# Grouped-query attention: one more chunk of scores exponentiated bank by bank, and VectorE's share of the exponentials begun three chunks earlier and ended three chunks later

## The chip, the cores and the metric

The kernel runs on one core of a Trainium2 chip. The metric is the device time of one execution in microseconds (us), the median of several executions.

## The reference

```
B, Hq, Hkv, Sq, Sk, D = 16, 32, 8, 288, 512, 128      # bf16
k, v = repeat(k, 4, axis=1), repeat(v, 4, axis=1)
p = softmax(einsum("bhqd,bhkd->bhqk", q, k) * D ** -0.5)
out = einsum("bhqk,bhkd->bhqd", p, v)
```

## The kernel before

There are 128 groups (batch x key head), each with 1152 queries against 512 keys. A group is cut into three chunks of 128 x 1536 scores, 384 chunks in all, numbered from 0. A chunk fills three banks of the matmul accumulator (PSUM). For chunk n, TensorE makes the scores; ScalarE exponentiates them into on-chip memory (SBUF); two chunks later TensorE multiplies with V, twelve matmuls that I call PV(n), with a column of ones in V for the denominators; VectorE divides and evicts. GpSimd copies each group's V, as it was transferred, into the layout with the column of ones.

In every sixth chunk VectorE exponentiates the last 120 columns itself, with eight instructions, and ScalarE gets 1416 columns. I call such chunks shared. The first chunks (and the last) go through ScalarE bank by bank, so that TensorE can go on before a whole chunk is done. The parts:

```
FIRST = 2            # chunks exponentiated bank by bank at the start
FIRST_SHARED = 6     # first shared chunk
EVERY = 6
...
def shared(n):
    return FIRST_SHARED <= n < NS - NC and (n - FIRST_SHARED) % EVERY == 0   # NS = 384, NC = 3
...
def op_exp(n):                       # ScalarE
    parts = [(0, CH)]                            # CH = 1536
    if shared(n):
        parts = [(0, CH - W)]                    # W = 120
    if n < FIRST or n == NS - 1:
        parts = [(x, x + BANK) for x in range(0, CH, BANK)]
    ...
def op_vc(g):                        # GpSimd: V of group g
    waits = [have("v", g)]                       # its transfer
    if g >= 2:
        waits.append(("s_pv", NC * (g - 2) + 2)) # PV of the second chunk of group g-2
    emit(eng, waits, lambda: eng.tensor_copy(v_sb[...], vd_sb[...]))
...
for r in range(NS - 1):              # VectorE, n = r + LAG, LAG = 2
    op_rc(r)                                     # reciprocals after PV(r)
    if shared(n):     op_y(n)                    # clamp, from PSUM
    if shared(n - 1): op_yu(n - 1, 1); op_yu(n - 1, 2); op_yp(n - 1)
    op_ev(r)                                     # eviction of r
    if shared(n):     op_yb(n); op_ym(n); op_yu(n, 0)   # from SBUF to SBUF
```

PV(r) waits, among others, for the eviction of r - 2, whose buffer it takes.

## Time and profile before

| | before |
|---|---|
| time, median | 521.98 us (521.74 to 523.07, 3 runs) |
| span of the profiled run | 520.0 us |
| busy: TensorE, ScalarE, VectorE, GpSimd | 98%, 99%, 71%, 15% |
| six chunks in the body | 7.982 us |

A period of six chunks is the repeating unit. I read it from the starts of TensorE's weight loads: the scores of chunk 13 begin at 21.69 us, those of chunk 373 at 500.64, and 478.95/60 = 7.982. The lines of the profile that carry the argument stand in the prediction below.

### The profile page before, as it was taken

The page shows a single profiled execution, that of the slowest core. Times are in us where ns is not written, and L with a number is a line of the kernel's source. Part 1 is how long each engine was busy: PE and PEld are TensorE (multiplying, and loading weights), DVE is VectorE, ACT ScalarE, POOL GpSimd, SP SyncE. Part 2 cuts the span into 40 slices and gives each one's busy share as a digit, 9 for nine tenths or more (in the row PEclk, how much of TensorE's full clock was granted, in tenths as well). Part 3 has the DMA queues.
Part 4 walks back from the last instruction along what each step waited for, and adds up shares of the span by engine and source line. Part 5 has one row for each costly group of instructions (what it writes and reads, how often), then busy time and mean ns, then how long its engine had stood idle before and what let it go on. Part 6 is the DMA issues. An engine that isn't in the chain of part 4 may idle for free.

```text
span 520.0 us, 15243 instructions
## 1 busy us (share of the span) xinstructions
PE 510.3 (98%) x6118; PEld 394.6 (76%) x6224; DVE 369.6 (71%) x1315; ACT 513.3 (99%) x393; POOL 79.8 (15%) x135
## 2 busy tenths in 40 slices
PE   8999999999999999999999999999999999999997
PEld 5777777777777777777777777777777777777776
DVE  2767767777777677676776776767767767677776
ACT  7999999999999999999999999999999999999997
POOL 2111111111111111111111111111111111111110
PEclk9999999999999999999999999999999999999999
DMA  9999999999999998999999989999998989998212
GB/s 186 237 218 230 267 194 248 225 213 210 219 233 256 208 245 201 235 248 240 215 241 209 209 225 220 241 185 209 229 240 232 227 194 201 192 234 198 86 69 93
DMA packets 253078, 110.06 MB, mean 212 GB/s; under 512 B 219728, under 2 KB 236752, under 8 KB 253008
## 3 DMA queue, kind: packets, MB, share of 16 engines
q1 hardware_dynamic: 252720, 108.82, 97.7%
q8 instruction: 49, 0.80, 0.7%
q10 hardware_dynamic: 288, 0.26, 0.2%
q14 instruction: 21, 0.17, 0.2%
HBM read 17.04 MB, written 37.75 MB: 105 GB/s over the span
## 4 chain that ended last, share of the span: by engine, by line
ACT 98%; DMA 1%; issue 1%; DVE 0%; PE 0%
ACT pt_sb L516 97%; DMA qt_sb<-in_q_dram 1%; ACT pt_sb L511 1%; PE ps_s L439 0%; DVE o_sb L585 0%; DVE o_sb L595 0%; PE ps_s L479 0%; DVE rl_sb L575 0%; PE ps_o L669 0%; DVE bad_sb L621 0%; DVE flag_i L734 0%; DVE bad_sb L618 0%
## 5 line engine op out<-in xcount | busy, mean ns | idle before, releaser
L516 ACT ACTIVATE pt_sb<-ps_s 128x1536 bf16<-128x1536 f32 (+2 forms) x384 | 508.8, 1441 | 0.0
L479 PE MATMUL ps_o<-v_sb,pt_sb 128*128 128x129 bf16 x4584 | 322.3, 220 | 1.1
L479 PEld LDWEIGHTS ps_o<-v_sb,pt_sb 128*128 128x128 bf16 x4584 | 282.8, 98 | 49.7 <-DVE o_sb L585 14.1
L439 PE MATMUL ps_s<-qt_sb,kt_sb 128*128 128x512 bf16 (+2 forms) x1430 | 290.4, 320 | 5.0 <-DMA qt_sb<-in_q_dram 0.5
L585 DVE TENSOR_TENSOR o_sb<-ps_o,rl_sb 128x384 bf16<-128x384 f32 x382 | 211.9, 555 | 9.3 <-DVE rl_sb L575 0.5
L439 PEld LDWEIGHTS ps_s<-qt_sb,kt_sb 128*128 128x128 bf16 x1536 | 123.9, 98 | 62.3 <-issue 1.1
L575 DVE RECIPROCAL rl_sb<-ps_o 128x3 f32<-128x3 f32 x382 | 68.1, 178 | 125.5 <-PE ps_o L479 124.0
L568 POOL COPY v_sb<-vd_sb 128x512 bf16<-128x512 bf16 x128 | 78.8, 616 | 429.1 <-PE ps_o L479 408.9
L549 DVE SCALAR_TENSOR_TENSOR u_sb<-u_sb,m_sb 128x120 f32<-128x120 f32 x126 | 35.6, 283 | 2.2
L556 DVE SCALAR_TENSOR_TENSOR pt_sb<-u_sb,e_sb 128x120 bf16<-128x120 f32 x63 | 17.8, 283 | 2.2
L549 DVE SCALAR_TENSOR_TENSOR u_sb<-m_sb 128x120 f32<-128x120 f32 x63 | 17.4, 277 | 0.0
L527 DVE TENSOR_SCALAR y_sb<-ps_o 128x120 f32<-128x120 f32 x63 | 15.9, 253 | 0.0
L540 DVE TENSOR_SCALAR m_sb<-t_sb 128x120 int32<-128x120 int32 x63 | 14.1, 223 | 2.2
L540 DVE TENSOR_SCALAR e_sb<-t_sb 128x120 int32<-128x120 int32 x63 | 13.6, 216 | 0.0
L450 PE MATMUL ps_o<-qt_sb,kt_sb 128*128 128x120 bf16 x63 | 13.6, 216 | 0.0
L533 DVE TENSOR_SCALAR t_sb<-y_sb 128x120 int32<-128x120 f32 x63 | 13.4, 213 | 0.0
L450 PEld LDWEIGHTS ps_o<-qt_sb,kt_sb 128*128 128x128 bf16 x63 | 6.2, 98 | 7.4
L511 ACT ACTIVATE pt_sb<-ps_s 128x512 bf16<-128x512 f32 x6 | 3.3, 616 | 2.3 <-PE ps_s L439 2.3
L411 DVE COPY kt_sb<-ps_o 128x128 bf16<-128x128 bf16 (+2 forms) x3 | 1.0, 336 | 6.2 <-PE ps_o L404 6.1
L613 DVE TENSOR_REDUCE st_sb<-rl_sb 128x1 f32<-128x72 f32 (+1 forms) x16 | 3.5, 216 | 0.0
L611 DVE TENSOR_REDUCE st_sb<-rl_sb 128x1 f32<-128x72 f32 (+1 forms) x16 | 3.5, 216 | 0.0
L417 PE MATMUL ps_o<-const-bfloat16-1.0 128*128 128x512 bf16 (+1 forms) x6 | 2.4, 570 | 0.9 <-PEq L752 0.9
(32 smaller groups left out, 12.0 us busy)
## 6 DMA issues: line engine op xcount, KB each, us to landing
out_dram<-o_sb SPq DMA_DIRECT2D x127, 288.0 KB, 3.7
vd_sb<-in_v_dram SPq DMA_DIRECT2D x31, 512.0 KB, 5.5
qt_sb<-in_q_dram SPq DMA_TRANSPOSE x128, 4.9
kt_sb<-in_k_dram SPq DMA_TRANSPOSE x32, 5.1
vd_sb<-in_v_dram SPq DMA_DIRECT2D x1, 384.0 KB, 4.6
out_dram<-o_sb SPq DMA_DIRECT2D x3, 96.0 KB, 1.6
kd_sb<-in_k_dram ACTq DMA_DIRECT2D x2, 128.0 KB, 2.7
vd_sb<-in_v_dram SPq DMA_DIRECT2D x1, 128.0 KB, 3.3
```

The lines of the kernel that those rows point to most:

```text
L439: ins = emit(eng, w_x, lambda: eng.matmul(ps_s[:, n % 2, c:c + w], kt_sb[:, sl, j, gi, :], qg[:, t * P:t * P + w], start=True, stop=True))
L450: emit(eng, [("s_ev", n - LAG - 1)], lambda: eng.matmul(ps_o[:, (n - LAG) % 2, BANK - W:BANK], kt_sb[:, (g // UG) % NSLOT, j, g % UG, :], ...
L479: ins = emit(eng, w_x, lambda: eng.matmul(outs(r)[:, t - r % NC * TPC, :], pt(g, t, j), v_sb[:, sl, gi * NJ + j, 0:DV], start=(x == 0), st ...
L516: emit(eng, waits, lambda: eng.activation(d, s, ACTF.Exp, scale=scale)).then_inc(sem["s_e"], 1)
L527: emit(eng, [("s_yb", nth(n) - NB), ("s_pv", n - LAG + 1)], lambda: eng.tensor_scalar(out=y_sb[:, b], in0=ps_o[:, (n - LAG) % 2, BANK - W: ...
L533: emit(eng, [("s_ym", 2 * (nth(n) - NB)), ("s_y", nth(n))], lambda: eng.tensor_scalar(out=t_sb[:, b], in0=y_sb[:, b], scalar1=Y_MUL, scala ...
L540: emit(eng, [("s_yp", nth(n) - NB), ("s_yb", nth(n))], lambda: eng.tensor_scalar(out=dst[:, b], in0=t_sb[:, b], scalar1=mask, scalar2=bits ...
L549: lambda: eng.scalar_tensor_tensor(out=u_sb[:, b, x], in0=src, scalar=QUARTIC[x], in1=m, op0=ALU.add, op1=ALU.mult)
L556: lambda: eng.scalar_tensor_tensor(out=pt_sb[:, n % NPT, CH - W:CH], in0=u_sb[:, b, 2], scalar=QUARTIC[3], in1=e_sb[:, b].bitcast(FP32), o ...
L568: emit(eng, waits, lambda: eng.tensor_copy(v_sb[:, sl, gi * NJ:(gi + 1) * NJ, 0:D], vd_sb[:, sl, gi].rearrange("p (j d) -> p j d", d=D))). ...
L575: emit(eng, [("s_pv", r + 1)], lambda: eng.reciprocal(rl_sb[:, TPC * r:TPC * (r + 1)].unsqueeze(2), outs(r)[:, :, D:DV])).then_inc(sem["s_ ...
L585: emit(eng, waits, lambda: eng.tensor_tensor(out=o_sb[:, g % NO, t0:t0 + TPC, :], in0=outs(r)[:, :, 0:D], in1=rl_sb[:, TPC * r:TPC * (r + ...
```

## The change

Two constants and one bound. The intent: chunk 2 lets TensorE go on sooner, and sharing begins at chunk 3 and ends at chunk 381, so ScalarE is relieved once more and earlier.

```diff
-    FIRST = 2
-    FIRST_SHARED = 6
+    FIRST = 3
+    FIRST_SHARED = 3
...
-            return FIRST_SHARED <= n < NS - NC and (n - FIRST_SHARED) % EVERY == 0
+            return FIRST_SHARED <= n < NS - 2 and (n - FIRST_SHARED) % EVERY == 0
```

## The prediction

> **What bounds the kernel now.** The work goes in 384 chunks of 128x1536 scores. For chunk n TensorE makes the scores (L439), ScalarE exponentiates them (L516), and two chunks later TensorE multiplies with V (L479). In every sixth chunk VectorE exponentiates the last 120 columns, so ScalarE gets 1416. I call chunks by number from 0; "PV(n)" is the product with V of chunk n.
>
> I read the page first. Its busy shares do not decide, and its chain names ScalarE:
>
> ```profile
> PE 510.3 (98%) x6118; PEld 394.6 (76%) x6224; DVE 369.6 (71%) x1315; ACT 513.3 (99%) x393; POOL 79.8 (15%) x135
> ...
> ACT 98%; DMA 1%; issue 1%; DVE 0%; PE 0%
> ```
>
> Two engines at 98 and 99% with nothing idle cannot both be the limit, so I looked at when instructions start, which the timeline of each engine gives. First ScalarE, from three windows of its timeline (start, length of the merged piece, how many instructions):
>
> ```profile
> 5.05 1.09 ACT L511 ACTIVATE pt_sb<-ps_s 128x512 bf16<-128x512 f32 x2 [2.33 <-PE ps_s L439]
> 6.02 0.60 ACT L516 ACTIVATE pt_sb<-ps_s 128x512 bf16<-128x512 f32 x1
> 6.50 1.10 ACT L511 ACTIVATE pt_sb<-ps_s 128x512 bf16<-128x512 f32 x2
> ...
> 7.93 2.85 ACT L516 ACTIVATE pt_sb<-ps_s 128x1536 bf16<-128x1536 f32 x2
> 10.59 2.88 ACT L516 ACTIVATE pt_sb<-ps_s 128x1536 bf16<-128x1536 f32 x2
> 13.26 2.80 ACT L516 ACTIVATE pt_sb<-ps_s 128x1416 bf16<-128x1416 f32 x2
> 15.95 2.79 ACT L516 ACTIVATE pt_sb<-ps_s 128x1536 bf16<-128x1536 f32 x2
> ```
>
> Chunks 0 and 1 go bank by bank: six pieces between 5.05 and 7.93 are 0.48 us from start to start. Chunks 2 to 5 start at 7.93, 9.26, 10.59, 11.93: 1.333 us each. So a piece of c columns costs ScalarE a fixed 0.053 us plus c x 0.833 ns when nothing holds it up (from (1.333 - 0.48)/1024 and the rest). By that, a chunk of 1416 takes 1.233 us (estimate). But chunks 6 and 7, the first of them short, take 15.95 - 13.26 = 2.69 us, where 1.233 + 1.333 = 2.57 would do: **ScalarE waits about 0.12 us after the short chunk.** A period of six chunks needs 5 x 1.333 + 1.233 = 7.90 us of ScalarE and takes
>
> ```profile
> 13.26 7.97 ACT pt_sb L516 x6
> 21.28 7.93 ACT pt_sb L516 x6
> ...
> 476.28 7.93 ACT pt_sb L516 x6
> ```
>
> (the chain of waits in order of time) (476.28 - 21.28)/57 = 7.982 us. So ScalarE has 0.08 us to spare in each period. What sets 7.982 is TensorE. Its timeline:
>
> ```profile
> 8.31 0.81 PE L439 MATMUL ps_s<-qt_sb,kt_sb 128*128 128x512 bf16 x3
> 8.96 0.94 PE L479 MATMUL ps_o<-v_sb,pt_sb 128*128 128x129 bf16 x12
> ...
> 13.04 0.88 PE L479 MATMUL ps_o<-v_sb,pt_sb 128*128 128x129 bf16 x12
> 13.76 0.81 PE L439 MATMUL ps_s<-qt_sb,kt_sb 128*128 128x512 bf16 x2
> 14.41 0.84 PE L479 MATMUL ps_o<-v_sb,pt_sb 128*128 128x129 bf16 x12
> 15.09 0.82 PE L439 MATMUL ps_s<-qt_sb,kt_sb 128*128 128x512 bf16 x6
> 15.74 0.84 PE L479 MATMUL ps_o<-v_sb,pt_sb 128*128 128x129 bf16 x12
> ```
>
> From 13.76 on it alternates 0.65 and 0.68 us without a gap: 1.33 us per chunk, six of them 7.98. An unhindered PV shows a length of 0.84. In the body all do; the two longer ones near the start, 0.94 and 0.88, are stalls of 0.10 and 0.04 us. The first is PV(1), whose last four matmuls need chunk 2 (they use its first two banks) and which waits for the whole exponential of chunk 2, ending 7.93 + 1.51 = 9.44; the second is PV(4), which waits in the same way for chunk 5 (11.93 + 1.54 = 13.47). **So: ScalarE bounds chunks 0 to 5, TensorE everything from about 13.7 us to the end.** At the very end PV(382) shows 1.11 instead of 0.84, a stall of 0.27 us on the second bank of chunk 383.
>
> **What the Trainium skill says.** "TensorE: Matmul & The Clock Gate", section "Back-to-back issue gap", gives N/2.4 + 2.5 ns for a warm matmul alone: 56.3 ns at 129 columns, 215.8 at 512. Then a chunk is 12 x 56.3 + 3 x 215.8 = 1323 ns; the trace has 1330. The trace agrees within 1%, and not with the shorter gap for long streams that the section also gives (131 ns at 512). "ScalarE: Activation LUTs", "What ACT_TABLE_LOAD costs", gives 186 ns + 0.833 ns per column for an ACTIVATE and an overlap of about 93 ns with its neighbour; slope and the length of a single bank agree (613 ns; the trace has 616), but the overlap here is 616 - 480 = 136 ns, and I use that. "Perfetto Trace Analysis", "Identifying the Most-Contended Engine", says that matmul occupancy does not tell how near TensorE is to its limit; that is why I read starts and not the 98%.
>
> **The change part by part.**
> 1. *Chunk 2 in three pieces.* ScalarE: 3 x 0.48 = 1.44 instead of 1.333, so +0.107 us, in the stretch that ScalarE bounds. TensorE: PV(1) may use the first two banks when they are done, at about 7.93 + 2 x 0.48 + 0.14 = 9.03 instead of 9.44, and needs them at 8.96 + 8 x 0.056 = 9.41: its stall of 0.10 goes. Scores of chunk 4 may overwrite bank by bank, too.
> 2. *The first shared chunk is 3, not 6.* ScalarE: -0.10 us at chunk 3, +0.10 at chunk 6. Sum for chunk 5: it starts at 7.93 + 1.44 + 1.233 + 1.333 = 11.94, before 11.93. So PV(4) waits for chunk 5 until the same moment as before. What PV(1) no longer waits is waited at PV(4): its stall grows from 0.04 to about 0.12-0.14. The scores of chunk 7 start at 13.76 before and at 13.76-13.77 after. **Gain at the start: 0.00 +- 0.03 us.** From there ScalarE starts chunk 7 at 14.60 at the earliest (13.27 + 1.333), where the scores let it start at 14.61; chunk 9 then gives it its slack.
> 3. *VectorE's work.* Shared chunks were 6 to 378 (63), now 3 to 381 (64): one more extra matmul (the same 120 columns, split off; +2.5 ns by the formula) and one more set of eight VectorE instructions: 0.25 + 0.21 + 0.22 + 0.22 + 0.28 + 2 x 0.28 + 0.28, about 2.0 us, on an engine with 29% to spare. In chunk 6, from VectorE's reading at 14.06 to its last result takes 2.4 us and the two delayed evictions end by 16.91 and 17.59, the next reciprocal coming at 17.95 on time; PV(7), which waits for the first of them, starts at 17.07 with 0.16 in hand. The same distances hold for chunk 3. There the reciprocal follows PV(1), ending near 9.80, and the eviction that PV(4) needs ends near 12.79, before 12.95.
> 4. *The end.* Chunk 381 being short gives ScalarE 0.10 us, but chunk 383 starts at 514.87, while its scores (issued 513.99, some 0.86 to ScalarE's start) allow 514.86: gain 0.01. The two evictions delayed by chunk 381's work would end at 515.8 and 516.5 instead of 515.0 and 516.3, and the reciprocal after PV(382) comes at about 516.47 either way, so the last stores hardly move: 0 to +0.05.
>
> One more short chunk is worth 0.10 us of ScalarE that TensorE does not let through. Sum: 0.00 (start) + 0.00 (body, TensorE's 1.33 per chunk is untouched) - 0.01 to +0.05 (end): about 0.0 us, 0.01% at most. I say 521.9 us, the median of before within its scatter.
>
> **The rivals.** (a) *ScalarE is the bound*, as the chain's 98% says: then 64 short chunks instead of 63 give -0.10, two more fixed costs +0.107, again zero, so the time does not tell the two apart; the chain does not either, since it follows ScalarE whenever that shows no idle time. (b) *TensorE keeps what PV(1) wins:* 0.10 to 0.13 us less, 521.85, if chunk 5 came earlier than I add up; the starts at 1.333 speak against. (c) *VectorE late:* if chunk 3's work held up PV(4) or chunk 381's the last evictions, 0.1 to 0.6 us more; for it speaks only the margin of 0.16. (d) *Phase:* shared chunks now fall on the other buffer of scores and apart from VectorE's reductions of every 24 chunks, whose period before (37.21 to 45.19) is as long as its neighbours, 7.98. So that gains nothing. Only a repeating effect could matter: 0.02 us in each of 64 periods would be 1.3 us, and even that is 0.25%.
>
> **Range and chances.** Three runs of before spread from 521.74 to 523.07, more than all terms above together. The range is 521.3 to 522.8: scatter on both sides and a tenth or two for (b) or (c). 2% is 10.4 us, a hundred times the largest term: within 2% 0.985, faster 0.01, slower 0.005.
>
> **What would show it.** PV(1) at 0.84 instead of 0.94; PV(4) at 0.95-0.98 instead of 0.88; scores of chunk 7 at 13.76 +- 0.03; chunk 3 starting near 9.37, chunk 5 near 11.94; periods of 7.98 in the body; PV(382) still near 1.1. Periods of 7.95 or 8.02 would prove the argument on the body wrong, PV(4) at 0.84 that on the start.

## The result, and the profile after

The changed kernel took 522.25 us (521.9 to 522.8, 4 runs), the kernel before 521.86 (521.69 to 523.07, 4 runs). The ratio of the fast runs is 1.0003, 95% interval 0.9986 to 1.0021: no difference by timing. The span of the profiled run went from 520.0 to 520.6 us.

The page of the changed kernel, engines' busy time and the chain that ended last:

```profile
PE 510.1 (98%) x6119; PEld 394.4 (76%) x6225; DVE 371.4 (71%) x1323; ACT 513.7 (99%) x395; POOL 79.8 (15%) x135
...
PE 96%; DVE 2%; issue 1%; DMA 1%
```

The busy shares are as before. The chain now runs through TensorE (96%), where before it ran through ScalarE (98%), though the time is the same. That is the sign of two engines near one limit: the chain takes whichever shows no gap, and tells little about which one binds.

TensorE's timeline in the changed kernel (start, length of the merged piece, how many):

```profile
7.72 0.40 PE L404 MATMUL ps_o<-ident,kd_sb 128*128 128x128 bf16 x4 [0.65 <-DMA kd_sb<-in_k_dram]
...
8.73 0.76 PE L439 MATMUL ps_s<-qt_sb,kt_sb 128*128 128x512 bf16 x3
9.32 0.21 PE L450 MATMUL ps_o<-qt_sb,kt_sb 128*128 128x120 bf16 x1
9.38 0.84 PE L479 MATMUL ps_o<-v_sb,pt_sb 128*128 128x129 bf16 x12
...
13.37 0.84 PE L479 MATMUL ps_o<-v_sb,pt_sb 128*128 128x129 bf16 x12
...
20.70 0.81 PE L439 MATMUL ps_s<-qt_sb,kt_sb 128*128 128x512 bf16 x3
21.66 0.85 PE L479 MATMUL ps_o<-v_sb,pt_sb 128*128 128x129 bf16 x12
```

Three things are to be seen. PV(1), at 9.38, is back at 0.84 us, as predicted (e2 will show that this need not be the pieces' doing). PV(4), at 13.37, is at 0.84 as well, where I had predicted a stall: TensorE had to wait for the second block of keys until 7.72 us (7.30 in the trace before), so it came too late to wait for ScalarE. And there is a gap that I had not predicted: the scores of chunk 12 start at 20.70 and need 0.65, so PV(10) could start at 21.35, but starts at 21.66. What held it, from the timeline of all engines:

```profile
19.39 0.66 POOL L568 COPY v_sb<-vd_sb 128x512 bf16<-128x512 bf16 x1 [4.50 <-DMA vd_sb<-in_v_dram]
19.49 0.69 DVE L549 SCALAR_TENSOR_TENSOR u_sb<-m_sb 128x120 f32<-128x120 f32 x1
...
21.05 0.55 DVE L585 TENSOR_TENSOR o_sb<-ps_o,rl_sb 128x384 bf16<-128x384 f32 x1
...
21.65 0.68 PEld L479 LDWEIGHTS ps_o<-v_sb,pt_sb 128*128 128x128 bf16 x12 [0.64 <-DVE o_sb L585]
```

PV(10) waits for the eviction that ends at 21.60. That eviction stands in VectorE's order behind the work for shared chunk 9, in which one instruction took 0.69 us that takes 0.28 elsewhere. It began while GpSimd copied V. In the kernel before no chunk is in work on VectorE at that moment; its copy at 19.54 harmed nothing.

So the theory to test was this. **Theory C:** starting the sharing earlier puts VectorE's work of chunks 3 and 9 where GpSimd's first copies of V fall, which follow the arrival of transfers and not the rhythm of the loop, and the two engines hold each other up. **Rival N:** that was chance. **Rival V:** VectorE's extra work alone is too long at the start. And for the body: **theory T**, TensorE bounds it, against **R**, ScalarE does.

### The profile page after: what moved, and what is told of

Its sections match the earlier page's. It is cut to its first block, busy times and chain, and to the rows that moved or that the text cites. A ratio compares the mean times of both kernels' runs of the same rounds, so it can differ in the third digit from the quotient of the medians.

```text
span 520.6 us, 15257 instructions
## 1 busy us (share of the span) xinstructions
PE 510.1 (98%) x6119; PEld 394.4 (76%) x6225; DVE 371.4 (71%) x1323; ACT 513.7 (99%) x395; POOL 79.8 (15%) x135
## 4 chain that ended last, share of the span: by engine, by line
PE 96%; DVE 2%; issue 1%; DMA 1%
PE ps_o L479 50%; PE ps_s L439 45%; DMA kd_sb<-in_k_dram 1%; PE ps_o L450 1%; PE ps_o L417 0%; DVE o_sb L585 0%; DVE u_sb L549 0%; PE ps_o L404 0%; DVE rl_sb L575 0%; DVE pt_sb L556 0%; DVE m_sb L540 0%; DVE o_sb L595 0%; DVE kt_sb L411 0%; DVE t_sb L533 0%; DVE y_sb L527 0%
## 5 line engine op out<-in xcount | busy, mean ns | idle before, releaser
L511 ACT ACTIVATE pt_sb<-ps_s 128x512 bf16<-128x512 f32 x8 | 4.4, 618 | 2.3 <-PE ps_s L439 2.3
```

## The experiments

Twelve runs were made. Two of them repeat a kernel (e1 and e12), and all but e6 gave right results. "Before" is the kernel before on the same chip. "Keys" is when TensorE began with the second block of keys; "3 to 13" the time from the scores of chunk 3 to those of chunk 13, which is 13.31 when nothing stalls; the last column one period of six chunks, from chunk 13 to 373. These three come from the starts of TensorE's weight loads in the one trace of each run. "Keys" follows the arrival of these keys, except in e7 and e11, where they landed at 7.76 and 5.93 us and TensorE came to them later.

| run | time | before | ratio (95%) | keys | 3 to 13 | six chunks |
|---|---|---|---|---|---|---|
| kernel before | | | | 7.30 | 13.41 | 7.982 |
| changed kernel | 522.25 | 521.86 | 1.0003 (0.9986, 1.0021) | 7.72 | 13.59 | 7.983 |
| e1 changed, again | 522.25 | 521.66 | 1.0011 (0.9997, 1.0025) | 7.38 | 13.99 | 7.983 |
| e2 sharing alone | 521.94 | 521.66 | 1.0005 (0.9992, 1.0019) | 7.33 | 14.01 | 7.983 |
| e3 banks alone | 521.74 | 521.66 | 1.0002 (0.9988, 1.0016) | 7.37 | 13.35 | 7.983 |
| e4 every twelfth shared | 523.68 | 521.66 | 1.0039 (1.0025, 1.0052) | 7.58 | 13.39 | 8.010 |
| e5 none shared | 527.41 | 521.79 | 1.0103 (1.0087, 1.0118) | 7.84 | 13.31 | 8.060 |
| e6 TensorE lighter | 520.47 | 521.79 | 0.9972 (0.9957, 0.9987) | 7.69 | 13.21 | 7.962 |
| e7 no copies | 522.96 | 521.79 | 1.0022 (1.0009, 1.0036) | 8.16 | 13.52 | 7.986 |
| e8 values early | 523.05 | 521.79 | 1.0021 (1.0007, 1.0035) | 8.80 | 13.30 | 7.983 |
| e9 copies twice | 536.73 | 522.00 | 1.0282 (1.0266, 1.0299) | 7.64 | 13.50 | 8.217 |
| e10 copies later | 521.99 | 522.00 | 0.9996 (0.9984, 1.0008) | 7.87 | 13.28 | 7.983 |
| e11 and keys early | 523.56 | 522.00 | 1.0027 (1.0013, 1.0041) | 8.42 | 13.87 | 7.983 |
| e12 copies later, again | 521.90 | 522.08 | 0.9996 (0.9982, 1.0011) | 7.71 | 13.28 | 7.983 |

### e1: the changed kernel again

No edit.

> The changed kernel itself, once more, for a second trace and a tighter interval. Theory T (TensorE sets 1.3305 us a chunk in the body; the start is set by the arrival of the second block of keys, 7.25 us in the trace before and 7.66 in the trace after): the six-chunk period is 7.98 us again, and the scores of chunk 7 start between 13.7 and 14.1 us, later or earlier with the arrival of the keys. Theory C (VectorE's 0.69 us instruction at 19.49 us, held up while GpSimd copied V, is tied to the new position of the shared chunks): PV(10) stalls by about 0.3 us again. Rival N (that hold-up was chance): PV(10) shows no stall. Time within 0.3 us of the kernel before in both cases.

The stall came back, and a larger one with it. TensorE's timeline, the copies on GpSimd's, and VectorE's in this run:

```profile
12.38 0.81 PE L439 MATMUL ps_s<-qt_sb,kt_sb 128*128 128x512 bf16 x3
13.55 0.85 PE L479 MATMUL ps_o<-v_sb,pt_sb 128*128 128x129 bf16 x12 [0.36 <-DVE o_sb L585]
```

```profile
10.51 1.17 POOL L568 COPY v_sb<-vd_sb 128x512 bf16<-128x512 bf16 x2 [4.75 <-DMA vd_sb<-in_v_dram]
```

```profile
10.65 0.55 DVE L533 TENSOR_SCALAR t_sb<-y_sb 128x120 int32<-128x120 f32 x1
11.23 0.52 DVE L540 TENSOR_SCALAR m_sb<-t_sb 128x120 int32<-128x120 int32 x1
...
12.94 0.55 DVE L585 TENSOR_TENSOR o_sb<-ps_o,rl_sb 128x384 bf16<-128x384 f32 x1
```

Two copies of V run back to back from 10.51 to 11.68, when V of groups 1 to 3 has arrived. In that stretch two steps of VectorE for chunk 3 take 0.55 and 0.52 us instead of 0.21 and 0.22, 0.64 us too much. The eviction ends at 13.49 and PV(4) starts at 13.55, where after its scores it could have started at 12.38 + 0.65 = 13.03. Note what the views show: VectorE is never idle here, and the wait is put down to the eviction, which itself has its usual 0.55 us. The held-up instruction is found only by its length. At PV(10) the trace shows a wait of 0.18 us more, where theory C had said 0.3. From chunk 3 to 13 it took 13.99 us, 0.59 more than in the trace before; and all five runs, 522.18 to 522.44, lie above all nine of before, 521.44 to 522.10, with medians 0.59 apart. The change costs about 0.1% here, though the interval of the ratio (0.9997 to 1.0025) still allows for no difference. N falls: the hold-up is there in both traces of the changed kernel.

### e2 and e3: each half of the change alone

```diff
-    FIRST = 3            # e2: sharing from 3 to 381, chunk 2 in one piece
+    FIRST = 2
```
```diff
-    FIRST_SHARED = 3     # e3: chunk 2 bank by bank, sharing from 6 to 378
+    FIRST_SHARED = 6     # and the bound NS - NC as before
```

> Shared chunks 3 to 381, but chunk 2 in one piece as before. T: the body is unchanged; at the start PV(1) waits for all of chunk 2 again (length 0.94 or so if the keys arrive by 7.3 us; nothing to see if they arrive at 7.7), chunk 5 starts 0.10 us earlier than in the kernel before, so PV(4) shows 0.84. Time equal to before within 0.3 us. C: PV(10) stalls as in the changed kernel, since the shared chunks lie as there. Rival R (ScalarE bounds): 0.10 us less than before.

> Chunk 2 in three pieces, shared chunks 6 to 378 as before. T: ScalarE is 0.107 us later at chunk 5 than before, so with keys at 7.3 us PV(4) ends its stall about 0.1 us later (length about 1.0), and the whole is 0.1 us longer than before; with keys at 7.7 us nothing shows. C: no stall at PV(10), since no shared chunk is in work there. R: plus 0.107 us in any case. All of this is at the edge of the timing, so the trace decides.

e2 shows the stalls of e1 (14.01 us from chunk 3 to 13; the first of VectorE's steps took 0.55 again), and its time is 0.28 above before, which is within the scatter; the profiled execution, at 522.30, was the slowest of its five. e3 shows none of them: 13.35, and a time level with before. So the stalls belong to the sharing, not to the banks. In e3 the stall seems to have moved as I had reckoned for that part: TensorE's timeline has PV(1) and PV(4) so:

```profile
9.03 0.84 PE L479 MATMUL ps_o<-v_sb,pt_sb 128*128 128x129 bf16 x12
...
13.02 0.91 PE L479 MATMUL ps_o<-v_sb,pt_sb 128*128 128x129 bf16 x12
```

0.94 became 0.84, and 0.88 became 0.91. But e2, with chunk 2 in one piece, shows PV(1) at 0.84 too, where I had expected 0.94: it started at 8.99, and ScalarE had begun 0.09 us earlier than in the trace before. So it is not shown that the pieces took away PV(1)'s stall. My figure of 1.0 for PV(4) was too high for this trace, and the expected loss of 0.1 us did not appear. The reason is in the starts: TensorE used the keys 0.07 us later than in the trace before, and ScalarE began its first chunk 0.12 us earlier (4.93 against 5.05). From its first start to that of chunk 5 ScalarE took 6.98 us against 6.88, so the 0.10 us that chunk 2 in pieces should cost it is there, and the earlier start hides it.

### e4, e5, e6: which engine bounds the body

```diff
-    EVERY = 6                    # e4
+    EVERY = 12
```
```diff
-    return FIRST_SHARED <= n < NS - 2 and ...      # e5
+    return False
```
```diff
     todo = sequence(r % NC)      # e6, on the kernel before; a wrong result on purpose
+    if r < NS - 2:
+        todo.pop(next(x for x in range(2, 6) if place(*todo[x])[1] != CH - P))
```

> The changed kernel with every twelfth chunk shared instead of every sixth (32 short chunks instead of 64). T: ScalarE needs 11 x 1.333 + 1.233 = 15.90 us per twelve chunks and TensorE 15.97, so TensorE still bounds: twelve chunks in 15.96 to 15.98 us, time within 0.3 us of the changed kernel. R (ScalarE bounds): 32 chunks get 0.10 us longer each, +3.2 us, some 525.4 us.

> The changed kernel with no shared chunk at all. Cost of a full chunk on ScalarE is what is asked. Theory S (ScalarE needs 1.343 us for each full chunk when it never waits, as the half-shared run suggests: 12 x 1.343 - 0.10 = 16.02 measured): six chunks take 8.06 us, the whole is some 4.8 us longer than before, 526.5. My recorded figure of 1.333: six chunks 8.00, +1.1 us. Theory R (ScalarE already bounds the kernel before): +6.3 us for 63 short chunks that are gone. No stalls at PV(4) and PV(10), as VectorE has no extra work.

> The kernel before with one of twelve matmuls left out of each product with V except the last two (a wrong result on purpose). TensorE then needs 1.274 us per chunk and must wait for ScalarE. S: six chunks take 6 x 1.343 - 0.10 = 7.96 instead of 7.98, the whole is 1.6 us shorter than before. My recorded slack of 0.08 us per six chunks: 7.90, 5.2 us shorter. If TensorE were the only limit: 6 x 0.056 = 0.34 us less per six chunks, 21 us shorter. R: no change at all.

e4 lies between the two expectations: twelve chunks take 16.02 us, not 15.97 (T) and not the 16.07 of R, which is 15.97 plus the 0.10 of one short chunk lost. That gave a new figure for ScalarE, (16.02 + 0.10)/12 = 1.343 us for a full chunk. e5 must then take 6 x 1.343 = 8.06 us, and took 8.060; the total, 5.6 us above before, exceeds the expected 4.8. In the trace, chunks 13 to 383 take 4.77 us more than in the trace before, as expected; the rest is a later start (0.54 us at the scores of chunk 3) and a longer end (0.84 us more from the scores of chunk 383 on). e6 must take 8.06 - 0.10 = 7.96, and took 7.962; its chain of waits, in order of time, steps by it:

```profile
21.49 2.60 ACT pt_sb L518 x2
29.45 2.60 ACT pt_sb L518 x2
37.41 2.60 ACT pt_sb L518 x2
```

With a twelfth of PV gone from TensorE the kernel gained 1.3 us and no more. So TensorE bounds the kernels before and after (7.98), and ScalarE stands 0.02 us per period behind it (7.96), not 0.08. R falls for the kernel with six chunks to a period; with twelve, it is ScalarE that binds.

### e7 and e8: the copies away, or at other times

```diff
     # e7: V of groups 1, 2 and 4 by a transfer straight into v_sb; GpSimd only passes the signal on
+    if g in (1, 2, 4):
+        emit(eng, [("s_vx%d" % g, 16)], lambda: eng.memset(tiny[:, g:g + 1], 0.0)).then_inc(sem["s_vc"], 1)
+        return
...
-    lambda: op_k(0, 2), lambda: op_v(0, None, 1, UG), lambda: op_q(2), ...
+    lambda: op_k(0, 2), lambda: op_direct(1), lambda: op_direct(2), lambda: op_v(0, None, 1, UG), lambda: op_direct(4), lambda: op_q(2), ...
```
```diff
     # e8: V of groups 1 to 3 before the keys of groups 2 and 3; V of groups 4 to 7 earlier
-    lambda: op_k(0, 2), lambda: op_v(0, None, 1, UG), lambda: op_q(2), lambda: op_q(3)
+    lambda: op_v(0, None, 1, UG), lambda: op_k(0, 2), lambda: op_q(2), lambda: op_v(1), lambda: op_q(3)
...  # op_v(1) is left out at its later place
```

> The changed kernel, with V of groups 1, 2 and 4 transferred straight to where TensorE reads it, so that GpSimd copies nothing at the times when VectorE works on chunks 3 and 9 (result stays right). C (VectorE's instructions of chunks 3 and 9 were held up by GpSimd's copies): VectorE's first step of chunk 3 from SBUF takes 0.21 us instead of 0.55, PV(4) and PV(10) show no stall, and the time is 0.3 to 0.7 us below the changed kernel, at that of the kernel before or 0.1 below. Rival V (VectorE's extra work is itself too long at the start): stalls as before.

> The changed kernel with two transfers of V asked for earlier (groups 1 to 3 before the keys of groups 2 and 3, groups 4 to 7 before a later block of queries), so that GpSimd's copies end before VectorE's steps of chunk 3 and wait for PV(7), not for the transfer, at chunk 9. C: no stall at PV(10), none or a smaller one at PV(4); time 0.2 to 0.6 us below the changed kernel. V: no difference.

In both, VectorE's first step of chunk 3 took 0.21 us and neither PV(4) nor PV(10) waited for an eviction; e8 went from chunk 3 to 13 in 13.30 us, the figure without any stall. VectorE in e7:

```profile
11.47 0.21 DVE L534 TENSOR_SCALAR t_sb<-y_sb 128x120 int32<-128x120 f32 x1
```

So far C held. But the times are 1.2 us above before, which I had not expected. The loss is at the start, and for two reasons. In e8, where a transfer of V went ahead of them, the second block of keys landed at 8.76 us (7.26 in the trace before). In e7 it landed at 7.76, but TensorE came to it only at 8.16, straight from the first scores:

```profile
4.48 3.90 PE L440 MATMUL ps_s<-qt_sb,kt_sb 128*128 128x512 bf16 x12 [0.49 <-DMA qt_sb<-in_q_dram]
8.22 0.39 PE L405 MATMUL ps_o<-ident,kd_sb 128*128 128x128 bf16 x4
```

The same twelve matmuls took 2.91 us in the trace before and 2.45 in e12. Those of 512 columns start 0.43 us apart to the last in e7 and e8; in the trace before that ends near 6.1 us, and in e12 they are 0.22 apart from the first on. The granted clock reads 0.999 or more in all four. No run tests what ends the slow stretch, so how much of the 1.2 us is due to the transfers is open. Besides, in e7 the scores of chunk 6 waited 0.24 us for queries, and a later copy of V, at 35.70, held up a step of chunk 21 (0.51 us). These two kernels are wins on the first stalls and losses on the start.

### e9: twice the copies, on the kernel before

```diff
             op_vc(g)
+            op_vc_again(g)       # the same copy into a spare tensor
...  # a slot of V is loaded anew only after both copies
```

> The kernel before; GpSimd does each copy of V a second time, into a spare tensor, right after the first, so that it reads and writes on-chip memory while VectorE does its steps of every shared chunk. C: VectorE's first step of a shared chunk takes some 0.5 to 0.6 us instead of 0.21 in all 63 of them, TensorE stalls 0.2 to 0.4 us in each period, and the time grows by 13 to 25 us. V (GpSimd does not hold up VectorE): no difference.

The groups of VectorE's instructions by line, kernel before and then e9 (busy us, mean ns):

```profile
L533 DVE TENSOR_SCALAR t_sb<-y_sb 128x120 int32<-128x120 f32 x63 | 13.4, 213 | 0.0
```

```profile
L534 DVE TENSOR_SCALAR t_sb<-y_sb 128x120 int32<-128x120 f32 x63 | 34.2, 543 | 0.0
L541 DVE TENSOR_SCALAR m_sb<-t_sb 128x120 int32<-128x120 int32 x63 | 14.1, 223 | 2.1
```

The step that falls on the second copy takes 0.54 us instead of 0.21 in all 63 shared chunks; the next, after the copy, is unchanged. The period grows from 7.982 to 8.217 us, and 0.235 x 63 = 14.8 is the whole difference in time (536.73 - 522.00 = 14.7). V falls: the same work of VectorE costs nothing or 0.23 us per shared chunk, depending on GpSimd alone.

The Trainium skill has this: "SBUF — State Buffer", section "Who interferes with whom", says that VectorE's second pair of ports is GpSimd's only pair, that instructions such as `tensor_scalar` can use it, and any with two inputs in SBUF its read port, and that the second to come is blocked until the first is done. The trace agrees: the steps from SBUF to SBUF wait (0.21 to 0.54 us, and 0.28 to 0.69 for one with two inputs), the eviction, which reads PSUM, does not (0.55 us during a copy too).

### e10, e12 and e11: mending it

```diff
     # e10, e12
-    waits.append(("s_pv", NC * (g - 2) + 2))
+    waits.append(("s_pv", NC * (g - 2) + 2 + (NC if g in (2, UG) else 0)))
```
```diff
     # e11: besides, the second block of keys asked for at once
-    for (s, n) in need(eng, [("s_k0", 2)]):
-        eng.wait_ge(s, n)
     op_kd(eng, 1)
```

> The changed kernel; GpSimd's copies of V for groups 2 and 4 wait three chunks longer (for PV(4) and PV(10)), the transfers stay in their order. C: of the two copies that ran back to back at 10.5 us only the first is left there, VectorE's second step of chunk 3 takes 0.22 us instead of 0.52 and its first at most 0.55, PV(4)'s stall falls from 0.6 us to 0.3 or less, PV(10)'s goes; from the scores of chunk 3 to those of chunk 13 it takes 13.3 to 13.6 us instead of 13.99, and the time is 0.4 to 0.7 us below the changed kernel, level with the kernel before. V: no difference.

> The run with later copies once more: in its first trace the second block of keys arrived only at 7.9 us, where no stall of PV(4) could be seen either way. C: whatever the arrival, 13.3 to 13.6 us from the scores of chunk 3 to those of chunk 13 (13.99 in the changed kernel's trace with keys at 7.4 us); time within 0.3 us of the kernel before.

> As the run with later copies, and the second block of keys is asked for at once, not after the first has been used. If its arrival (7.3 to 7.7 us) sets when TensorE can start chunk 3, the scores of chunk 3 start earlier than 8.3 us, at 8.0 or so, where the exponentials of chunk 1 allow it, and the whole gains up to 0.3 us, unless the two transfers of keys and the first queries slow each other: then the first scores start after 4.4 us and it loses as much.

With two copies moved by three chunks, e12's GpSimd and VectorE show:

```profile
10.29 0.61 POOL L568 COPY v_sb<-vd_sb 128x512 bf16<-128x512 bf16 x1 [4.37 <-DMA vd_sb<-in_v_dram]
14.27 1.17 POOL L568 COPY v_sb<-vd_sb 128x512 bf16<-128x512 bf16 x2 [3.37 <-PE ps_o L479]
```

```profile
10.98 0.21 DVE L533 TENSOR_SCALAR t_sb<-y_sb 128x120 int32<-128x120 f32 x1
11.23 0.22 DVE L540 TENSOR_SCALAR m_sb<-t_sb 128x120 int32<-128x120 int32 x1
```

Nothing is held up, chunk 3 to 13 takes 13.28 us in both traces, and both runs are level with the kernel before (0.9996 each). That is the mended change, with the stalls gone and nothing gained: what the prediction said of the change itself. In both traces the keys came late (7.7 and 7.9 us), so how much of PV(4)'s stall would remain with early keys is open. e11 was a miss: with the second block of keys asked for at 1.29 us instead of 4.30, the first queries landed at 6.14 instead of 4.38 (e12), the first scores started at 6.18 instead of 4.4, and the time rose by 1.6 us. Its 13.87 from chunk 3 to 13 is no hold-up of VectorE, whose first two steps took 0.21 and 0.22 us: PV(1) and PV(3) stalled (0.97 and 1.02 us) on ScalarE, which had begun at 6.61 instead of 4.85 (e12). No version with a right result beat the kernel before.

## Why the prediction was right or wrong

**The time: right.** 521.9 predicted, 522.25 measured, inside 521.3 to 522.8; "within 2%" held. The reason given, that TensorE's 1.33 us per chunk in the body is untouched, held too: 7.982 before, 7.983 after, and e6 shows that ScalarE would not allow less than 7.962.

**TensorE as the bound, ScalarE with 0.08 us to spare: right in kind, wrong in size.** The failing term is "1.333 us each" for a full chunk on ScalarE; it is 1.343 (e5), and the slack is 0.02. I took the starts of chunks 2 to 5 as ScalarE's own pace. But the lengths of those four instructions grew from 1.51 to 1.54 us, so their ends were 1.343 apart. In e5, where ScalarE never waits, the lengths stay at 1.55 us and the starts are 1.343 apart; why the lengths grow before that no run shows. "Perfetto Trace Analysis", section "Per-instruction lifecycle: what the profiler-reported window actually captures", says that such an instruction's start is when it begins to execute and its end when its last write is acknowledged; with overlapping instructions the pace has to be read at both ends.

**Chunk 2 in three pieces: mostly not shown.** "Its stall of 0.10 goes": it went (PV(1) at 0.84), but it went in e2 as well, without the pieces. "Its stall grows from 0.04 to about 0.12-0.14" at PV(4), on account of ScalarE, could not be seen: in the first trace TensorE had come late from the keys, and in e1 the eviction held PV(4) up longer. e3, the half without these effects, shows 0.07, and there ScalarE's 0.10 us for the pieces is found. What my sum lacked is that the start itself moves by more than any of its terms: TensorE began with the second block of keys between 7.30 and 7.87 us in kernels that ask for it alike.

**VectorE's work: the step that failed.** "The same distances hold for chunk 3 ... the eviction that PV(4) needs ends near 12.79, before 12.95." It ended at 13.49 in e1. I had copied VectorE's distances from chunk 6, where GpSimd's copy had just ended; at chunk 3 two copies ran beside VectorE's steps, and at chunk 9 one. Rival (c), "VectorE late", is what happened, with its 0.1 to 0.6 us, though not by the margin I gave as the reason: TensorE waited 0.70 us for evictions in e1 and 0.31 in the first trace, and from chunk 3 to 13 that made 0.59 and 0.19 us more than in the trace before. It cost no more because in these two traces only the first two shared chunks meet copies that wait for transfers. From then on a copy starts with the reciprocal after PV, and ends just before VectorE's first step from SBUF (14.60 against 14.69 at chunk 6 of the trace before, and 0.08 to 0.09 us before it in all 63 of its shared chunks). The prediction did not know of this margin. That it holds at the new places too, and so that the total came out right, is luck: e9 takes the margin away and loses 14.7 us.

**The end: right within the scatter.** From the scores of chunk 383 to the end of the span it took 5.94 us against 5.99, where -0.01 to +0.05 was predicted; e1 and e2, with the same end, differ by 0.12. PV(382) shows 1.07 instead of 1.11.

**Phase, rival (d): right.** The other buffer and the reductions changed no period.

## What to carry to other kernels

When work is moved to an earlier place in a pipelined loop, its durations at the new place are not those of the steady state: look there for what runs beside it, above all what follows arriving transfers. An instruction that is held up by a port shows as a longer instruction, not as a wait, so compare lengths of the same line (0.21 became 0.54 us), not only gaps. And where two engines are within a per cent of each other, relieving the one that does not bind is worth nothing (one short chunk more for ScalarE, with the stalls mended: e10 at 521.99 us against 522.00), and relieving the one that does is worth only the slack of the other (e6: 1.3 us of the 21 that TensorE saved). The chain of waits does not tell which it is; a run that lightens one of them does.

## What the Trainium skill lacked or had wrong

- "SBUF — State Buffer" has the shared ports right, but neither it nor another page that I read says how it looks in a profile: the blocked time lies inside the reported length of the instruction (0.21 became 0.54 us in 63 of 63), and the wait that TensorE shows for it names a later, undisturbed instruction (0.36 us at PV(4), put down to the eviction).
- "ScalarE: Activation LUTs": the overlap of neighbouring ACTIVATEs is given as about 93 ns; here it was larger: 103 to 164 ns for the single banks at the start of the trace before, and in e5, where ScalarE never waits, 204 ns (1547 ns long, starts 1343 apart).
- "TensorE: Matmul & The Clock Gate": of the two figures for a stream of 512-column matmuls, the formula N/2.4 + 2.5 ns holds (a chunk in 1330 ns against 1323), the 131 ns for long streams does not: three of them take 0.65 us in the body, 217 ns each.
- No page that I read gives the scatter or the mutual delay of first transfers: the same request, made at 4.2 to 4.5 us, landed 3.0 to 3.5 us later in eleven traces, and one request of 128 KB made 3 us earlier (e11) moved the landing of the first queries from 4.38 to 6.14 us.
